# A gate's row sums: from the seam between two stages into the attention heads, in half blocks

## The chip, the cores and the metric

The kernel runs on one core of one Trainium2 chip. The metric is the device time of one execution in microseconds (us). Three runs of the kernel before gave 2838.04, 2838.57 and 2839.91 us; their median, 2838.57 us, is the time that the change is compared with. Everything else comes from one more execution that was profiled: it took 2840.08 us, of which the profile shows a span of 2838.3 us from the first to the last instruction.

The engines are named as in the profile: PE is the matmul engine (PEld its weight loads), DVE the vector engine, ACT the scalar engine, POOL is GpSimd, SP the engine from whose queue most transfers are issued.

## The reference

One input `x` (2048 tokens, 1024 features, float32) goes through two attention blocks of 32 heads, 32 wide, and the results are mixed row by row by a gate:

```python
x = A_x
g = _sigmoid((x * gate_w).sum(-1, keepdims=True))     # one number for each token
a = _A_ref(x, A_wqkv, A_wo)     # linear attention: phi(q) (phi(k)^T v) / (phi(q) . sum phi(k)), then @ wo
b = _B_ref(x, B_wqkv, B_wo)     # softmax attention, then @ wo
return g * a + (1 - g) * b
```

with `phi(t) = where(t > 0, t + 1, exp(t)) + 1e-6`. The gate's sum over 1024 features is a small part of the arithmetic: 2 million products against the matmuls of two attention blocks.

## The kernel before, in words

Every matmul operand of the projections is split into a high and a low part, and three products replace one (`three`, lines 151 to 157: high times high, high times low, low times high). Tokens are cut into 16 blocks of 128 (`NT`), features into pieces of 512 (`C`).

The work has these stages, by the time in the profile:

- **0 to about 400 us, the first stage.** The softmax block's queries, keys and first values are projected, split and stored to DRAM; a split copy of `x` goes to DRAM as `xs`.
- **about 400 to 525 us, the seam.** The remaining value chunk of the softmax block (`kind == "v"` in `linear`) is projected in 16 units of one token block. Each unit needs 1 MB of `xs` from DRAM (`load_half`: half a unit at a time into three halves of `big4` and `xh`), gives one store of values (`v_out`), and the row maxima of the first head start (`maxima`, the matmul of line 1131 and the DVE reduce of line 1136). The first heads' queries and keys are loaded on POOL's queue (`load_first`), their values with `load_v`, a gather of rows of 128 bytes.
- **525 to about 1720 us, the heads along the linear attention's keys and values** (`kind == "kv"`, 64 units), **to about 2120 us along its queries** (`"q"`), and then **along its output** (`"o"`). For each of the 32 heads, scores are computed twice: once with tokens on partitions for the row maxima (line 1131, reduced by DVE on line 1136), once transposed (line 1305) and put through Exp by ACT (line 1308) into a tile of 2048 columns; line 1462 multiplies these with the values. The rows' sums of the probabilities are added up by POOL, in adds of 1536 columns (lines 1393 and 1397), and for the last 512 columns by DVE in a PSUM bank (lines 1411 and 1413).
- **to the end, the output** projection of the softmax block and the mix.

All engine orders are written by a planner in the kernel: `T[...]` holds a planned time for each engine, `use(engine, cost)` advances it, streams (`lin`, `max`, `head`, `out`) are Python generators, and the main loop picks the one that can go on at the planned PE time. Small DVE work is put off with `defer(fn, at, cost, rank)` and fitted by `fill` where the planned DVE has room; the lowest rank goes first. Six to seven PSUM banks go round between the matmuls and their readers (`take`, `give`). SP and each engine execute their own orders strictly in sequence, so an instruction that waits holds up what stands behind it.

The gate, before, is a generator of its own (`gate`, lines 487 to 500), advanced by the seam's units from the third on: it loads the weights (spread over the partitions) into `zrep` on POOL's queue, and then for each of the 16 token blocks a whole block of `x` (128 x 1024, 512 KB), two buffers deep (`big12`), also on POOL's queue. One DVE instruction (line 495) multiplies the block with the weights and puts the row sums into a column of `g_sb`. At the end ACT and DVE make g and 1 - g of it (`omg_sb`). The first reader of `g_sb` is the linear attention's query stage (line 1048), that of `omg_sb` the output (line 1552).

Of the kernel before, what the change touches and what calls it, by code (L numbers as in the profile page):

```python
# [37 lines left out]
SLACK = 0.4  # L38
DMA_ISSUE = 0.45
WARM = 8  # L40
WO_STEP = 4
LATE = 1.0
MANUAL = {ET.PE, ET.DVE, ET.Activation, ET.SP, ET.Pool}
# [4 lines left out]
def kernel(  # L48
# [435 lines left out]
        store(1, 0, U2, H21)  # L484
        next(side, None)

    def gate():
        xn = halves_of(big_tile(12, F32))
        junk = halves_of(big_tile(13, F32))[0]
        nc.gpsimd.dma_start(zrep, bass.AP(tensor=gate_w.tensor, offset=gate_w.offset, ap=[[0, P], [1, D]]))  # L490
        for t in range(NT):
            nc.gpsimd.dma_start(xn[t % 2], x[t * P:(t + 1) * P, :])
            yield
            use("dve", 1.2)
            nc.vector.scalar_tensor_tensor(junk, xn[t % 2], 1.0, zrep, op0=ALU.mult, op1=ALU.mult,
                                           accum_out=g_sb[:, t:t + 1])
        nc.scalar.activation(g_sb, g_sb, AF.Exp, scale=-1.0)
        nc.vector.tensor_scalar_add(g_sb, g_sb, 1.0)
        nc.vector.reciprocal(g_sb, g_sb)
        nc.vector.tensor_scalar(omg_sb, g_sb, -1.0, 1.0, op0=ALU.mult, op1=ALU.add)  # L500

    def halves_of(t):
        return [t[:, i * D:(i + 1) * D] for i in range(2)]
# [429 lines left out]

    def linear():
        extra = iter(())
        gates = gate()
        for n, (i, t) in enumerate(units):
            kind, c = chunks[i]
            follow = chunks[i + 1] if i + 1 < len(chunks) else None
            lag = 2 if kind == "v" else 0  # L940

            def renew(k):

                mark = Later(None, 0.0, 0.0, 0, None)
                w_left[k][:] = [mark]
                next_w.append((follow, k, mark, nc.vector if kind == "v" else nc.gpsimd))
                pump_w(kind == "v")

            yield bank_at
            b = take()  # L950
            ps = bank[b]
            T["pe"] = max(T["pe"], free[b])
            lin_kind[0] = kind
            if (kind, c, t) in (("q", 1, 2), ("q", 1, 8), ("o", 0, 2), ("o", 0, 8)):
                load_mix()
            for k in range(NK):
                yield lambda: ended(w_left[k], w_ready[k], xp_ready.get(2 * n + k // HK, 0.0))
                need(w_left[k])
                if n < TPC:
                    stat = [xpiece(1, xname(0, k % 2), p, k // 2)[:, t * P:(t + 1) * P] for p in range(2)]  # L960
                else:
                    stat = [xstat_lin(n, k, p) for p in range(2)]
                for m, _ in enumerate(three(ps, stat, (wpart(k, 0), wpart(k, 1)), k)):
                    lin_pe(1.0)
                    if m < 2:
                        yield always
                store_mix()
                if kind == "v":
                    if n in (4, 5) and k == 0:
                        load_v(n - 4)  # L970
                    if t > 1 and (k == 3 or k == 7 and t % 2):
                        next(gates, None)
                if n == 1 and k == 0:
                    for m in range(2 * TPC, 2 * TPC + 3):
                        load_half(m)
                if k % HK == HK - 1 and 2 * n + k // HK >= 2 * TPC:
                    load_half(2 * n + k // HK + 3)
                if k == 0 and n + 7 == len(units) and not o_main[0]:
                    load_o(0)
                if k == 1 and n + 1 == len(units):  # L980
                    assert finished[0] >= H - 2
                    need(pr_left[extra_pr[2]])
                    xo_t[0] = big_tile(PR[extra_pr[2]], F32R)
                    split_o(0, slice(0, NK - 1))
                if k == NK // 2 and n + 1 == len(units) and over["head"]:
                    split_o(1, slice(0, NK - 1))
                if k == NK - 1:
                    yield from extra
                if follow and follow[0] == "o":
                    if t == NT - 1:  # L990
                        w_left[k].clear()
                        yield lambda: 0.0 if mixed.count((k // HK, follow[1])) == 8 * HK else None
                        load_wa(follow[1], k)
                    continue
                if follow and t == NT - 2 and k == 0:
                    yield lambda: None if mix_here or stores else 0.0
                if follow and t == NT - 2 and k < min(LEAD_W, NK):
                    coming_w.append(load_w(*follow, k, LEAD_W + 1))
                if follow and t == NT - 1 and k >= lag:
                    renew(k - lag)  # L1000
            extra = iter(())
            e, r = mid[3 + n % 3], mid[6]
            if kind == "v":
                give(b, use("act", 0.5, T["pe"] + LATENCY["pe"]))
                v_out(c, token(i, t), ps, mid[11 - n % 2])
            elif kind == "kv":
                va = mid[7][:, (n % 2) * HC:(n % 2 + 1) * HC]
                yield from keys_alone(n - 2)
                nc.scalar.copy(va, ps[:, HC:])
                use("act", 0.28, T["pe"] + LATENCY["pe"])  # L1010
                end = phi(ps, e, HC)

                def more(end, c=c, t=t, e=e, ps=ps):
                    pk = e[:, :HC]
                    nc.vector.scalar_tensor_tensor(pk, pk, 1.0, ps[:, :HC], op0=ALU.min, op1=ALU.add)
                    z_end[c % 2] = use("pool", 0.69, end)
                    if t == 0:
                        nc.gpsimd.tensor_copy(zsum[c % 2], pk)
                    else:
                        nc.gpsimd.tensor_add(zsum[c % 2], zsum[c % 2], pk)  # L1020

                todo = [defer(more, end, 0.34)]
                give(b, 0.0, todo)
                keys(n, c, t, e, va, todo)
                if t == NT - 1:
                    extra = keysum(c)
            elif kind == "q":
                yield from keys_alone(n - 3)
                yield lambda: None if n - 3 not in turned and chunks[units[n - 3][0]][0] == "q" else 0.0
                end = phi(ps, e, C)  # L1030
                d = dn[n % 2]

                def sums(_, e=e, ps=ps):
                    nc.vector.scalar_tensor_tensor(ps, e, 1.0, ps, op0=ALU.min, op1=ALU.add)

                def scaled(_, c=c, ps=ps, r=r):
                    nc.vector.tensor_mul(r, ps, zrep[:, c * C:(c + 1) * C])

                last = []

                def dens(end, r=r, d=d, last=last):
                    nc.vector.tensor_reduce(d, r.rearrange("p (h d) -> p h d", d=DH), AX.X, ALU.add)
                    nc.scalar.add(d, d, eps)
                    last[0].at = use("act", 0.2, end)

                def divide(_, t=t, e=e, ps=ps, d=d):
                    nc.vector.reciprocal(d, d)
                    nc.vector.scalar_tensor_tensor(
                        e.rearrange("p (h d) -> p h d", d=DH), ps.rearrange("p (h d) -> p h d", d=DH),
                        g_sb[:, t:t + 1], d.unsqueeze(2).to_broadcast([P, C // DH, DH]),  # L1050
                        op0=ALU.mult, op1=ALU.mult)

                todo = chain(((sums, 0.63), (scaled, 0.63), (dens, 0.63), (divide, 0.9)), end)
                last.append(todo[-1])
                give(b, 0.0, todo)
                tasks.append((lambda todo=todo: None if kv_todo else both(ended(todo + o_left), o_free[(len(turned) + 1) % 2], bank_at()),
                              lambda n=n, c=c, t=t, e=e, todo=todo: queries(n, c, t, e, todo)))
            else:
                res = mid[(7, 10)[n % 2]]
                give(b, use("act", 0.5, T["pe"] + LATENCY["pe"]))  # L1060
                nc.scalar.copy(res, ps)
                dma(ra_d[t][:, c * C:(c + 1) * C], res)
            if follow and follow[0] != "o" and t == NT - 1:
                for k in range(NK - lag, NK):
                    renew(k)
# [584 lines left out]
    while streams or tasks:  # L1650
        if not begun[0] and lin_done[0] >= warm and s_done[0] >= NT * NJ + LEAD:
            begun[0] = True
            advance("head")
        pump_w()
        fold_now()
        add_now()
        load_all(False)
# [77 lines left out]
```

## Time and profile before

| | |
|---|---|
| median of three runs | 2838.57 us (2838.04 to 2839.91) |
| the profiled execution | 2840.08 us, span 2838.3 us, mean granted PE clock 0.999 |
| PE busy | 2820.7 us (99%), 15944 matmuls |
| DVE busy | 2231.1 us (79%), 3659 instructions |
| POOL busy | 1936.0 us (68%) |
| ACT busy | 1596.9 us (56%) |
| transfers | 424.36 MB, mean 150 GB/s |

The views used are: the totals by engine; stretches (busy time of each engine between two times, with the granted PE clock, the share of time in which the 16 DMA engines moved packets, and GB/s); groups of instructions by line (busy us, mean ns of one, idle time of the engine just before them and who ended it); waits (who waited for whom, total us, times, longest); the instructions of one tile; and the timeline. Busy time counts an instruction from start to end. Matmuls overlap, so each shows 390 ns although one of 512 columns starts every 0.227 us.

### The profile page before, as it was taken

To read this page: it belongs to the slowest core of one execution; us is meant where nothing else is said; L and a number is where in the kernel's file an instruction comes from. 1 tells how busy PE (TensorE), PEld (TensorE's weight loads), DVE (VectorE), ACT (ScalarE), POOL (GpSimd) and SP (SyncE) were. 2 spreads that over 40 slices of the span, in tenths; PEclk is the share of its full clock that TensorE was granted. 3 is DMA by queue.
4 is the path that set the end of the run, shared out by engine and by line. 5 is a ranking of instruction groups with operands and counts; after the bars stand their busy time and mean duration, and the time that the engine had idled before them with its cause. 6 is when DMAs were issued, how large, how long until landed. Compare 5 with 4: busy or idle time off the path is not lost.

```text
span 2838.3 us, 46552 instructions
## 1 busy us (share of the span) xinstructions
PE 2820.7 (99%) x15944; PEld 2055.4 (72%) x15944; DVE 2231.1 (79%) x3659; ACT 1596.9 (56%) x2994; POOL 1936.0 (68%) x947
## 2 busy tenths in 40 slices
PE   9999999999999999999999999999999999999999
PEld 8888887676677667776777767776766666776787
DVE  7777747788888888888888888778888888887522
ACT  5334320566676667666666666666666656666400
POOL 0000041599999989999999999889889888885000
PEclk9999999999999999999999999999999999999999
DMA  8867768433344334333433344454666455544642
GB/s 274 252 220 231 217 208 283 136 101 103 99 122 109 99 94 127 100 97 105 125 103 102 100 124 142 143 183 161 201 185 174 135 160 142 153 113 129 202 148 78
DMA packets 373928, 424.36 MB, mean 150 GB/s; under 512 B 104750, under 2 KB 210478, under 8 KB 373692
## 3 DMA queue, kind: packets, MB, share of 16 engines
q1 hardware_dynamic: 356396, 396.21, 45.6%
q0 software_dynamic: 17296, 25.17, 4.7%
q8 instruction: 127, 2.08, 0.3%
q14 instruction: 109, 0.89, 0.1%
HBM read 293.86 MB, written 112.98 MB: 143 GB/s over the span
## 4 chain that ended last, share of the span: by engine, by line
PE 97%; DMA 2%; DVE 0%; POOL 0%; ACT 0%; issue 0%; SPq 0%; ACTq 0%; POOLq 0%; DVEq 0%
PE bank L1305 17%; PE bank L1131 16%; PE bank L1462 16%; PE bank L152 15%; PE bank L155 15%; PE bank L157 15%; DMA big<-in_x 1%; PE bank L1196 1%; PE bank L919 1%; PE bank L808 0%; DMA big<-qk 0%; DMA big<-wa 0%; PE bank L1188 0%; DMA extra<-in_a_wqkv 0%; PE bank L879 0%; DMA big<-xs 0%
## 5 line engine op out<-in xcount | busy, mean ns | idle before, releaser
L1397 POOL TENSOR_TENSOR big<-big,big 128x512 f32<-128x512 f32 (+2 forms) x694 | 1644.3, 2373 | 116.5 <-ACT big L1308 74.0
L1136 DVE TENSOR_REDUCE mx<-bank 128x1 f32<-128x512 f32 x2048 | 1304.5, 683 | 254.9 <-PE bank L1131 250.8
L1308 ACT ACTIVATE big<-bank 128x512 f32<-128x512 f32 x2048 | 1179.6, 601 | 431.6 <-PE bank L1305 362.7
L1131 PE MATMUL bank<-big,big 128*128 128x512 f32 x1888 | 740.3, 392 | 2.6 <-ACT big L1308 1.8
L1305 PE MATMUL bank<-big,big 128*128 128x512 f32 x1888 | 742.1, 394 | 0.7 <-ACT mid L355 0.6
L152 PE MATMUL bank<-big,big 128*128 128x512 f32 x1608 | 628.4, 391 | 2.9 <-DMA big<-xs 2.9
L157 PE MATMUL bank<-big,big 128*128 128x512 f32 x1604 | 625.6, 390 | 2.3 <-DMA big<-xs 2.3
L155 PE MATMUL bank<-big,big 128*128 128x512 f32 x1608 | 627.2, 390 | 0.0
L1462 PE MATMUL bank<-big,mid 128*32 128x512 f32 x4096 | 454.1, 593 | 0.0
L1305 PEld LDWEIGHTS bank<-big,big 128*128 128x128 f32 x1888 | 354.0, 188 | 126.5 <-issue 46.9
L1131 PEld LDWEIGHTS bank<-big,big 128*128 128x128 f32 x1888 | 354.7, 188 | 79.0 <-ACT big L1308 5.2
L152 PEld LDWEIGHTS bank<-big,big 128*128 128x128 f32 x1608 | 302.5, 188 | 69.3 <-DMA big<-xs 3.7
L157 PEld LDWEIGHTS bank<-big,big 128*128 128x128 f32 x1604 | 301.3, 188 | 65.6 <-DMA big<-xs 3.2
L155 PEld LDWEIGHTS bank<-big,big 128*128 128x128 f32 x1608 | 302.4, 188 | 63.3 <-DVE big L294 0.2
L1462 PEld LDWEIGHTS bank<-big,mid 128*32 128x32 f32 x4096 | 142.6, 110 | 265.2 <-issue 265.2
L1088 POOL MEMSET big<- 32x512 f32 (+1 forms) x4 | 3.9, 973 | 383.7 <-PE bank L157 383.7
L1413 DVE TENSOR_TENSOR bank<-bank,big 128x512 f32<-128x512 f32 x364 | 251.6, 691 | 5.3 <-ACT big L1308 3.6
L152 PE MATMUL bank<-big,xh 128*128 128x512 f32 x376 | 148.4, 395 | 3.0 <-DMA xh<-xs 2.6
L155 PE MATMUL bank<-big,xh 128*128 128x512 f32 x376 | 147.8, 393 | 0.2 <-DMA big<-wa 0.2
L157 PE MATMUL bank<-big,xh 128*128 128x512 f32 x376 | 147.3, 392 | 0.0
L1393 POOL TENSOR_TENSOR big<-big,big 128x1536 f32<-128x1536 f32 (+1 forms) x31 | 122.8, 3960 | 35.7 <-ACT big L1308 35.7
L1471 ACT COPY mid<-bank 128x512 f32<-128x512 f32 x32 | 18.8, 588 | 207.5 <-PE bank L1462 200.7
(129 smaller groups left out, 2003.4 us busy)
## 6 DMA issues: line engine op xcount, KB each, us to landing
big<-xs SPq DMA_DIRECT2D x288, 256.0 KB
big<-qk SPq DMA_DIRECT2D x690, 64.0 KB
xh<-xs SPq DMA_DIRECT2D x144, 256.0 KB
qk<-mid SPq DMA_DIRECT2D x128, 256.0 KB
big<-oA SPq DMA_DIRECT2D x84, 256.0 KB
xs<-big SPq DMA_DIRECT2D x64, 256.0 KB
oA<-mid SPq DMA_DIRECT2D x64, 256.0 KB
big<-big POOLq DMA_DIRECT2D x50, 256.0 KB, 5.6
```

Source lines behind the costliest of these rows:

```text
L152: yield nc.tensor.matmul(ps, sh, mh_, start=(kt == 0), stop=False)
L155: yield nc.tensor.matmul(ps, sh, ml_, start=False, stop=(late and last))
L157: yield nc.tensor.matmul(ps, sl, mh_, start=False, stop=last)
L919: nc.tensor.transpose(pt[:, i * P:(i + 1) * P], pq[:, i * P:(i + 1) * P], ident)
L1131: nc.tensor.matmul(bank[b], q[:, t % TPC * P:(t % TPC + 1) * P], k[:, j * C:(j + 1) * C], start=True, stop=True)
L1136: nc.vector.tensor_reduce(m[:, t, j:j + 1], bank[b], AX.X, ALU.max)
L1305: nc.tensor.matmul(bank[b], k[:, t * P:(t + 1) * P], q_cols(h, j), start=True, stop=True)
L1308: nc.scalar.activation(pr_t[i][:, j * C:(j + 1) * C], bank[b], AF.Exp, scale=SCALE)
L1393: nc.gpsimd.tensor_add(lacc[:, :qp], pr(0)[:, :qp], pr(1)[:, :qp])
L1397: nc.gpsimd.tensor_add(lacc[:, sl], lacc[:, sl], pr(t)[:, sl])
L1413: nc.vector.tensor_add(lacc[:, qp:] if t == NT - 1 else l_b[:, :n], l_b[:, :n], src)
L1462: nc.tensor.matmul(av_b[j * DH:(j + 1) * DH, :], v[:, t, :], pr(t)[:, j * C:(j + 1) * C], start=(t == 0), stop=(t == NT - 1))
```

## The change: what it does

The generator `gate` and its calls go. A function `gate_step` is called once in each turn of the planner's main loop and acts while the linear stream is in its keys and values. Its first call issues two loads of the weights (128 x 512 each) into `mid8` and `mid9` on SP's queue. Each step then loads one half block of `x` (128 x 512, 256 KB) into `mid10`, also on SP's queue, and defers one DVE instruction to at least 9 us (planned) later, at a planned cost of 0.9 us and with rank 2. It multiplies in place and puts the row sums of the first half into `g_sb`, of the second into `omg_sb`. The next step may come 12 us after that instruction. After 32 steps DVE adds the two halves, and the four instructions that follow are the same as before. `zrep`, `big12` and `big13` are no longer used for the gate.

```diff
+GATE_STEP = 12.0
...
-    def gate():
-        xn = halves_of(big_tile(12, F32))
-        junk = halves_of(big_tile(13, F32))[0]
-        nc.gpsimd.dma_start(zrep, bass.AP(tensor=gate_w.tensor, offset=gate_w.offset, ap=[[0, P], [1, D]]))
-        for t in range(NT):
-            nc.gpsimd.dma_start(xn[t % 2], x[t * P:(t + 1) * P, :])
-            yield
-            use("dve", 1.2)
-            nc.vector.scalar_tensor_tensor(junk, xn[t % 2], 1.0, zrep, op0=ALU.mult, op1=ALU.mult,
-                                           accum_out=g_sb[:, t:t + 1])
-        nc.scalar.activation(g_sb, g_sb, AF.Exp, scale=-1.0)
...
+    gate_w_t = [mid[8], mid[9]]
+    gate_at, gate_n = [0.0], [0]
+
+    def gate_step():
+
+        n = gate_n[0]
+        if lin_kind[0] != "kv" or gate_at[0] is None or gate_at[0] > T["pe"] or n > 2 * NT:
+            return
+        if n == 0:
+            for i, w in enumerate(gate_w_t):
+                dma(w, bass.AP(tensor=gate_w.tensor, offset=gate_w.offset + i * C, ap=[[0, P], [1, C]]))
+        gate_n[0] += 1
+        if n == 2 * NT:
+            nc.vector.tensor_add(g_sb, g_sb, omg_sb)
+            nc.scalar.activation(g_sb, g_sb, AF.Exp, scale=-1.0)
...
+            use("dve", 0.4)
+            return
+        t, i = divmod(n, 2)
+        xn, to = mid[10], (g_sb, omg_sb)[i]
+        dma(xn, x[t * P:(t + 1) * P, i * C:(i + 1) * C])
+        gate_at[0] = None
+
+        def part(end):
+            nc.vector.scalar_tensor_tensor(xn, xn, 1.0, gate_w_t[i], op0=ALU.mult, op1=ALU.mult,
+                                           accum_out=to[:, t:t + 1])
+            gate_at[0] = end + GATE_STEP
+
+        defer(part, T["pe"] + 9.0, 0.9, 2)
...
     def linear():
         extra = iter(())
-        gates = gate()
...
-                    if t > 1 and (k == 3 or k == 7 and t % 2):
-                        next(gates, None)
...
         pump_w()
+        gate_step()
         fold_now()
```

In the built programs the PE has the same instructions before and after. Their order is the same up to the first head's transpose of maxima (profiled at 500 us) and again from the query stage on; between them single instructions change places by a few positions, and in one spot a matmul of a projection by some sixty. DVE has 32 products of 128 x 512 in place of 16 of 128 x 1024, and one add more. POOL's queue loses 17 transfers, SP's gains 34.

More of the change, by code (lines that the diff above doesn't have):

```diff
@@ L485, in quad @@
         next(side, None)
-    def gate():
-        xn = halves_of(big_tile(12, F32))
-        junk = halves_of(big_tile(13, F32))[0]
-        nc.gpsimd.dma_start(zrep, bass.AP(tensor=gate_w.tensor, offset=gate_w.offset, ap=[[0, P], [1, D]]))
-        for t in range(NT):
-            nc.gpsimd.dma_start(xn[t % 2], x[t * P:(t + 1) * P, :])
-            yield
-            use("dve", 1.2)
-            nc.vector.scalar_tensor_tensor(junk, xn[t % 2], 1.0, zrep, op0=ALU.mult, op1=ALU.mult,
-                                           accum_out=g_sb[:, t:t + 1])
-        nc.scalar.activation(g_sb, g_sb, AF.Exp, scale=-1.0)
-        nc.vector.tensor_scalar_add(g_sb, g_sb, 1.0)
-        nc.vector.reciprocal(g_sb, g_sb)
-        nc.vector.tensor_scalar(omg_sb, g_sb, -1.0, 1.0, op0=ALU.mult, op1=ALU.add)
+    gate_w_t = [mid[8], mid[9]]
[11 more added lines that the diff above has]
+            nc.scalar.activation(g_sb, g_sb, AF.Exp, scale=-1.0)
+            nc.vector.tensor_scalar_add(g_sb, g_sb, 1.0)
+            nc.vector.reciprocal(g_sb, g_sb)
+            nc.vector.tensor_scalar(omg_sb, g_sb, -1.0, 1.0, op0=ALU.mult, op1=ALU.add)
+            use("dve", 0.4)
[9 more added lines that the diff above has]
+        defer(part, T["pe"] + 9.0, 0.9, 2)
     def halves_of(t):
@@ L1027, in linear @@
             elif kind == "q":
+                assert gate_n[0] > 2 * NT
                 yield from keys_alone(n - 3)
```

## The prediction

> **What bounds the kernel now.** I read the totals first, then stretches, to find where the PE isn't busy; then its waits there, the transfers behind them, and, for the place that the work moves to, the groups of DVE and POOL.
>
> ```profile
> PE 2820.7 (99%) x15944; PEld 2055.4 (72%) x15944; DVE 2231.1 (79%) x3659; ACT 1596.9 (56%) x2994; POOL 1936.0 (68%) x947
> ...
> core 0: us, PE busy (x) PEld busy (x) DVE busy (x) ACT busy (x) POOL busy (x), PEclk, DMA share, GB/s
> 420.00:450.00 30.00, 23.02 (x84) 17.05 (x83) 10.85 (x18) 2.01 (x4) 4.36 (x9) 0.89 0.92 283
> 450.00:498.00 48.00, 48.00 (x213) 39.74 (x212) 46.35 (x77) 3.53 (x6) 4.23 (x8) 1.00 0.83 275
> 498.00:530.00 32.00, 27.50 (x116) 20.89 (x116) 20.72 (x38) 12.53 (x23) 2.18 (x2) 1.00 0.66 212
> 530.00:1720.00 1190.00, 1189.71 (x7625) 834.89 (x7624) 1035.47 (x1752) 797.05 (x1545) 1116.29 (x555) 1.00 0.39 105
> ```
>
> The PE sets the time: 2820.7 us busy. The change leaves its instructions as they are, so time can come only from gaps. The seam has one from 420 to 450 us, 30 - 23.02 = 6.98 us, with the clock at 0.89 and the transfers at 0.92 of their engines. From 530 us on, along the keys and values, the PE has no gap, DVE is 87% busy (1035.47 of 1190) and POOL 94% (1116.29).
>
> ```profile
> engine line waited for: us in total, times, longest us
> PE bank L152 <- DMA big<-xs: 2.9, 2, 1.6
> PE bank L1131 <- ACT big L1308: 1.8, 1, 1.8
> PE bank L152 <- DMA xh<-xs: 2.6, 1, 2.6
> PE bank L157 <- DMA big<-xs: 2.3, 1, 2.3
> PE bank L1131 <- DVE mx L1136: 0.7, 1, 0.7
> ...
> 420.47 1.06 POOL L492 DMA_DIRECT2D big<-in_x  x2 [0.34 <-issue]
> 428.69 0.53 POOL L492 DMA_DIRECT2D big<-in_x  x1 [7.17 <-DMA big<-in_x]
> ...
> 420.65 1.22 SPq L169 DMA_DIRECT2D mid<-v  x1
> ...
> 429.74 0.57 SPq L169 DMA_DIRECT2D mid<-v  x1
> ...
> L169 SPq DMA_DIRECT2D big<-xs x8: 319/383/7076, 428.3 to 448.5; - x8
> L169 SPq DMA_DIRECT2D xh<-xs x4: 386/410/5622, 422.1 to 438.5; - x4
> ...
> L169 SPq DMA_DIRECT2D big<-xs x167: 319/341/1715, 530.1 to 1685.7; - x167
> L169 SPq DMA_DIRECT2D xh<-xs x84: 319/344/772, 554.3 to 1691.6; - x84
> ```
>
> In the seam the PE waits for `xs`, the operand of its own units. Two of these loads needed 5.6 and 7.1 us only to be issued; in the stage after it, the same loads never need over 1.7. Both stand on SP's queue right behind a gather of values in rows of 128 bytes (`mid<-v`, 420.65 and 429.74 us), while on POOL's queue the gate's blocks of 512 KB run from 420 us on: the transfer engines are shared.
>
> **The seam: what goes.** The gate's 17 transfers leave the seam. The 6.98 us of gap fall away as far as they come from them. To this comes the clock: after the 2.63 us wait the matmuls run at half pace.
>
> ```profile
> 427.35 0.39 PE L157 MATMUL bank<-big,big 128*128 128x512 f32 x1
> 430.38 0.79 PE L152 MATMUL bank<-big,xh 128*128 128x512 f32 x1 [2.63 <-DMA xh<-xs]
> ...
> 433.52 0.54 PE L155 MATMUL bank<-big,xh 128*128 128x512 f32 x1
> 433.90 0.39 PE L157 MATMUL bank<-big,xh 128*128 128x512 f32 x1
> 434.13 0.39 PE L152 MATMUL bank<-big,xh 128*128 128x512 f32 x1
> ```
>
> From 430.38 to 433.90 eight matmuls start, 0.44 us apart; from 433.90 to 434.13 it is 0.23. That costs 8 x 0.21 = 1.7 us for such a gap, and the stretch's 0.89 (11% of 30 us) is 3.3 us for all. At most 6.98 + 3.3 = 10.3 us can be won. DVE's 16 products (1220 ns, below) also go; the 0.7 us wait for `mx` L1136 was theirs. What is late next: the gather and the unit's own loads remain, so some of the gap may. I take 9.5 us; the ends are 5 (half of it, if the gather by itself still holds SP up once) and 10.3. The instruction order of the PE is the same up to 500 us, so nothing new comes in between. The waits from 498 to 530 us (4.5 us) are for `xs` beside the next weights and for ACT, when the gate has ended: they stay, earlier by what was won.
>
> **Along the keys and values: what comes.** First, 34 issues on SP's queue. An issue takes 0.34 us (the median of `xs` loads), 12 us in 1190, and each holds up what stands behind it, loads of `xs`, queries, keys and weights, by that much. The transfer share there is 0.39. The first load of `x` waits for the value store from `mid10`, and behind it on SP's queue stand the third head's queries and half a unit of `xs`:
>
> ```profile
> 521.01 0.32 SPq L169 DMA_DIRECT2D v<-mid  x1
> 524.52 0.80 SPq L169 DMA_DIRECT2D extra<-qk  x2
> ```
>
> Those queries were issued 3.5 us after that store already before, since their tile had to come free, so the wait is covered. Without that cover half a unit of `xs` comes a microsecond later, with two halves in hand. Cost: nothing. By the times of their neighbours in the trace, the DVE products stand 5 to 31 us behind the place of their load in the built order, mostly over 8; the loads of twice the size landed in 6.0 us (median) in the full seam:
>
> ```profile
> big<-in_x POOLq DMA_DIRECT2D x16, 512.0 KB, 6.0
> ```
>
>  So DVE waits for none of them. (If it did, all reduces queue behind it.)
>
> Second, 32 DVE products with a read of the accumulator, and these rows are for them, and for what they meet:
>
> ```profile
> L495 DVE SCALAR_TENSOR_TENSOR big<-big,zrep 128x1024 f32<-128x1024 f32 x16 | 19.5, 1220 | 38.5 <-DMA big<-in_x 38.5
> L739 DVE TENSOR_TENSOR big<-mid,big 128x512 fp32r<-128x512 f32 x6 | 4.2, 693 | 9.6 <-ACT big L737 9.6
> ...
> L495 DVE DVE_READ_ACCUMULATOR big<-big,zrep 128x1 f32 x16 | 1.3, 82 | 0.0
> ...
> L1136 DVE TENSOR_REDUCE mx<-bank 128x1 f32<-128x512 f32 x1197 | 756.6, 682 | 140.2 <-PE bank L1131 138.6
> L1413 DVE TENSOR_TENSOR bank<-bank,big 128x512 f32<-128x512 f32 x263 | 181.7, 691 | 2.3 <-ACT big L1308 1.3
> L1206 DVE RECIPROCAL bank<-bank 128x128 f32<-128x128 f32 x72 | 69.4, 964 | 1.8
> L1015 DVE SCALAR_TENSOR_TENSOR mid<-mid,bank 128x256 f32<-128x256 f32 x64 | 26.5, 414 | 3.8 <-ACT bank L790 3.4
> ...
> L1397 POOL TENSOR_TENSOR big<-big,big 128x1536 f32<-128x1536 f32 x188 | 661.7, 3520 | 38.2 <-ACT big L1308 28.0
> L1397 POOL TENSOR_TENSOR big<-big,big 128x512 f32<-128x512 f32 x216 | 276.5, 1287 | 13.0
> L1393 POOL TENSOR_TENSOR big<-big,big 128x1536 f32<-128x1536 f32 x19 | 74.3, 3913 | 7.0 <-ACT big L1308 7.0
> ```
>
> An instruction of 128 x 512 takes 0.69 us and the read 0.08: 0.77, under the planned 0.9, so 0.13 spare. 32 x 0.77 = 25 us fit into DVE's 155 us of idle time, and the planner has set the PE's order for them. By itself that costs the PE nothing.
>
> But each product reads two tiles of SBUF, its block and the weights, while POOL is adding for 94% of the time. Through this whole stage DVE does nothing of the kind: its large groups each have a `bank`, which is PSUM, among the operands; and line 495 ran in the seam, where POOL adds nothing (4.23 us busy in 48, all transfer issues). So no row shows a price. From below it is nothing: L1413, with one SBUF operand, takes 691 ns here, as L739 does with POOL idle. From above, the two take turns: the product starts only when the running add ends. At a random moment the rest of an add is the sum of n d²/2 over 1190 us: 188 x 3.52²/2 + 216 x 1.287²/2 + 19 x 3.913²/2 = 1489, or 1.25 us; 32 x 1.25 = 40 us of DVE. What of this reaches the PE hangs on the banks. I paired the 1197 reduces of L1136 with the next matmul into their bank, in instruction order: half of the matmuls start at most 0.67 us after the reduce's end. With the spare 0.13, what goes over 0.8 us is paid: 188 x 2.72²/2 + 216 x 0.487²/2 + 19 x 3.113²/2 = 813, or 0.68 us; times 32, 22 us. Where DVE idles anyway (138.6 of 1190 us, 12%) it is covered: 19 us stay. Behind the waiting product stand the reduces; behind them the matmuls of L1131 that need their banks, and all else on the PE.
>
> [...]
>
> Gaps of 2.3 us or more I charge with the half clock, after the 2.63 us row: rests over 3.1 us are (188 x 0.42 + 19 x 0.81)/1190 = 8% of 32, 2.5 gaps, 1.7 us each: 4.3 us. [...] POOL waits too, 32 x 0.69 = 22 us of its 74 idle: covered.
>
> Third, the closing add and the four small operations, on 16 columns, under 0.3 us each, with a wait for ACT among them: 1 us, once.
>
> **The sum**, on the profiled 2840.08 us: - 9.5 + 19 + 4.3 + 1 = + 14.8, 2854.9. The median of the runs was 1.5 us under the profiled execution: 2853.4, said as 2853.
>
> **The rivals.**
>
> *Beside each other.* DVE's second operand costs POOL and itself nothing. For: all present DVE forms run undisturbed beside the adds. Against: none of them reads twice from SBUF. Then the seam's 9.5 us are won and the small stage end is paid: 2838.57 - 9.5 + 1 = 2830, faster. It decides at 9.5/32 = 0.3 us of PE time for each product: under that the change wins.
>
> *Partial turns.* Both slow down a little, or the planner's places happen to fall between adds; 0.3 us a product: 2838.57 - 9.5 + 9.6 + 1 = 2840, no change.
>
> *Long waits.* POOL's adds stand in line, and if the product lost against the next add as well, its wait would be 3.5 us longer for each: 32 x 3.5 = 112 us more, 2965. Against: an add and a product of one add's rest is the simpler order, and ACT gates POOL often (28.0 us of waits).
>
> *The seam's loads stay late.* The gather alone then blocks SP: 5 us won instead of 9.5, which moves every case up by 4.5.
>
> **How the numbers follow.** 0.2% of 2838.57 is 5.7 us, about what a measurement here can tell from nothing. Between its ends of 0 and 1.25 us, a product costs more than (9.5 + 5.7)/32 = 0.48 us in six tenths of the interval and less than 0.12 us in one. The lower end is a way of its own, though, so I move weight to it. Turns 0.55; beside 0.28; partial 0.13; long 0.04. Faster 0.28, same 0.13, slower 0.59. The range: low 2828, the whole 10.3 us won and nothing paid; high 2870, turns with no bank slack (40 x 0.88 + 4.3 + 1 - 9.5 = + 31). Long waits lie outside. Turns alone: 2844 to 2870.
>
> **What would show it.** Right: in the seam the waits for `xs` and the clock's 0.89 gone; along the keys and values the new DVE product's idle time before it ended by POOL, or its duration at 2 us and more, and waits of L1131 for `mx` L1136 adding up to some 20 us. Wrong: a product of 0.7 us with POOL's adds at 3.52 us beside it (the first rival), issues of 5 us still there in the seam (the fourth), or DVE waiting for `in_x` (a cost that I set to nothing).

## The result, and the profile after

The changed kernel took 2845.14 us (median, 2842.17 to 2847.33), the kernel before 2839.87 us beside it (2837.35 to 2841.56): a ratio of 1.002, with a 95% interval from 1.0011 to 1.0029. It is slower, as forecast, but by 5.3 us where the forecast said 14.4. The profiled execution took 2845.76 us, 5.7 more than that of before.

The totals of the changed kernel, then its stretches (the same columns as in the prediction):

```profile
PE 2824.3 (99%) x15944; PEld 2051.5 (72%) x15944; DVE 2267.2 (80%) x3692; ACT 1598.1 (56%) x2994; POOL 1937.3 (68%) x930
```
```profile
core 0: us, PE busy (x) PEld busy (x) DVE busy (x) ACT busy (x) POOL busy (x), PEclk, DMA share, GB/s
420.00:450.00 30.00, 30.00 (x134) 24.71 (x133) 15.50 (x23) 2.35 (x4) 0.00 (x0) 1.00 0.73 208
450.00:498.00 48.00, 48.00 (x214) 39.64 (x213) 37.40 (x57) 5.08 (x10) 0.00 (x0) 1.00 0.57 181
...
530.00:1440.00 910.00, 903.40 (x5782) 626.58 (x5784) 822.87 (x1381) 601.21 (x1163) 849.25 (x422) 1.00 0.42 113
1440.00:1500.00 60.00, 57.76 (x340) 38.89 (x333) 51.93 (x90) 35.70 (x71) 56.23 (x28) 0.97 0.37 97
530.00:1720.00 1190.00, 1181.16 (x7548) 819.07 (x7547) 1066.97 (x1792) 782.96 (x1516) 1107.20 (x549) 1.00 0.41 111
```

The seam's gap is gone (30.00 busy at clock 1.00, before 23.02 at 0.89). Along the keys and values the PE now has 8.8 us without a matmul (1190 - 1181.16, before 0.3). DVE is busy 31.5 us longer there than before.

The groups of DVE and POOL along the keys and values, by form, and all products of the gate taken together (shortest, median and longest in ns, first and last start):

```profile
L1152 DVE TENSOR_REDUCE mx<-bank 128x1 f32<-128x512 f32 x1187 | 746.6, 682 | 105.0 <-PE bank L1147 104.0
L514 DVE SCALAR_TENSOR_TENSOR mid<-mid,mid 128x512 f32<-128x512 f32 x32 | 55.3, 1728 | 0.0
...
L1413 POOL TENSOR_TENSOR big<-big,big 128x1536 f32<-128x1536 f32 x187 | 663.0, 3545 | 42.9 <-ACT big L1324 33.0
L1413 POOL TENSOR_TENSOR big<-big,big 128x512 f32<-128x512 f32 x216 | 278.9, 1298 | 13.2
```
```profile
L514 DVE SCALAR_TENSOR_TENSOR mid<-mid,mid x32: 703/1418/3720, 518.3 to 1464.8; 128x512 f32<-128x512 f32 x32
```

A product takes 1728 ns in the mean, not 0.69 us; POOL's adds keep their length (3545 and 1298 ns, before 3520 and 1287). DVE pays for the meeting.

The PE's waits from 420 to 1720 us, and SP's issues from 420 to 450 us:

```profile
PE bank L1147 <- DVE mx L1152: 5.9, 5, 2.2
PE bank L1321 <- DVE kvb L835: 1.7, 1, 1.7
...
PE bank L153 <- DMA big<-xs: 0.9, 1, 0.9
```
```profile
L170 SPq DMA_DIRECT2D big<-xs x12: 319/362/2977, 424.4 to 448.7; - x12
L170 SPq DMA_DIRECT2D xh<-xs x6: 320/382/1135, 421.7 to 441.3; - x6
```

The waits for `xs` have shrunk to 0.9 us and the issues of 5.6 and 7.1 us are gone; of the waits for DVE, that for `mx` has grown (7.4 us in all, before 0.7) and that for `kvb` is new. DVE waits for `in_x` nowhere.

Named waits don't hold all that the PE loses, since a matmul shows 0.39 us and the next starts 0.227 us after it, so that a start late by less than the difference shows no gap. So I count **lost pitch**: for every matmul of 512 columns on the lines of the projections and scores, the time to the next start less 0.227 us, summed by stretch (us; one profiled execution each; the last four are experiments below; of the stretch from 498 to 530 us a difference of 3 us says little, since the changed kernel and close_act execute the same instructions there and lost 6.3 and 9.2):

| stretch | before | changed | no_gate | one_input | cost2 | close_act |
|---|---|---|---|---|---|---|
| 420 to 450 | 11.5 | 0.0 | 1.1 | 1.5 | 0.2 | 0.8 |
| 498 to 530 | 6.2 | 6.3 | 3.8 | 3.7 | 3.6 | 9.2 |
| 530 to 1440 | 11.2 | 23.3 | 11.4 | 12.7 | 17.3 | 22.2 |
| 1440 to 1500 | 0.9 | 5.3 | 0.9 | 4.8 | 0.9 | 1.1 |
| 1500 to 1725 | 2.7 | 2.8 | 2.5 | 2.8 | 10.6 | 3.0 |

Before to changed: -11.5 in the seam, +12.1 where 30 of the 32 products run, +4.4 at the closing (from 1473 us on): +5.2 with the small rest, against 5.3 in the medians.

### The profile page after: what moved, and what is told of

The parts are those of the page before. It is cut to its first block, busy times and chain, and to the rows that moved or that the text cites. A ratio compares the mean times of both kernels' runs of the same rounds, so it can differ in the third digit from the quotient of the medians.

```text
span 2844.0 us, 46559 instructions
## 1 busy us (share of the span) xinstructions
PE 2824.3 (99%) x15944; PEld 2051.5 (72%) x15944; DVE 2267.2 (80%) x3692; ACT 1598.1 (56%) x2994; POOL 1937.3 (68%) x930
## 4 chain that ended last, share of the span: by engine, by line
PE 95%; DVE 4%; DMA 1%; issue 0%; ACT 0%; SPq 0%; ACTq 0%
PE bank L1321 16%; PE bank L1147 16%; PE bank L153 15%; PE bank L156 15%; PE bank L158 15%; PE bank L1478 15%; DVE mx L1152 2%; DVE mid L514 1%; PE bank L937 1%; PE bank L1212 1%; DMA big<-wa 0%; PE bank L826 0%; DVE bank L1222 0%; DVE bank L1429 0%; PE bank L1204 0%
## 5 line engine op out<-in xcount | busy, mean ns | idle before, releaser
L1413 POOL TENSOR_TENSOR big<-big,big 128x512 f32<-128x512 f32 (+2 forms) x694 | 1651.5, 2384 | 122.7 <-ACT big L1324 80.0
L1478 PE MATMUL bank<-big,mid 128*32 128x512 f32 x4096 | 454.1, 593 | 0.0
L1147 PEld LDWEIGHTS bank<-big,big 128*128 128x128 f32 x1888 | 354.9, 188 | 87.2 <-DVE mx L1152 10.4
L1478 PEld LDWEIGHTS bank<-big,mid 128*32 128x32 f32 x4096 | 142.3, 110 | 265.4 <-issue 265.4
```

The costliest lines, as they stand in the source:

```text
L1147: nc.tensor.matmul(bank[b], q[:, t % TPC * P:(t % TPC + 1) * P], k[:, j * C:(j + 1) * C], start=True, stop=True)
L1413: nc.gpsimd.tensor_add(lacc[:, sl], lacc[:, sl], pr(t)[:, sl])
L1478: nc.tensor.matmul(av_b[j * DH:(j + 1) * DH, :], v[:, t, :], pr(t)[:, j * C:(j + 1) * C], start=(t == 0), stop=(t == NT - 1))
```

## The experiments

The theory is that of the prediction: a seam that gains, products that take turns with POOL's adds, a closing that costs something. Its rival is that the two engines run beside each other and the loss is the order's or the transfers'. Differences below are against the runs of before on the same chip (2838.79, 2838.97 and 2838.46 us in the three groups).

**no_gate: the seam by itself.** The gate is left out: g and 1 - g are two constants of 0.5.

```diff
-        if lin_kind[0] != "kv" or gate_at[0] is None or gate_at[0] > T["pe"] or n > 2 * NT:
-            return
+        if n == 0:
+            gate_n[0] = 2 * NT + 1
+            nc.vector.memset(g_sb, 0.5)
+            nc.vector.memset(omg_sb, 0.5)
+        return
```


> The gate is left out: g and 1 - g are set to 0.5 once, no load of x or of the gate's weights for it and no product anywhere. If the seam's gap came from the gate and everything that the change pays comes from the gate's own instructions, the seam from 420 to 450 us has no gap and the stretch along the keys and values is as in the kernel before: some 11.4 us under the kernel before, 2828 us, 17 us under the changed kernel. If the new order of the PE or other things cost the time along the keys and values, it is less: 2833 us or more.

Measured: 2826.02 us, ratio 0.9952 (0.9939 to 0.9964), 12.8 us under before. The seam is worth that much, and 530 to 1440 us is back at 11.4 us of lost pitch.

**one_input: the same place and loads, one operand.** The product becomes a plain sum over the half block; the weights are left out of it.

```diff
-            nc.vector.scalar_tensor_tensor(xn, xn, 1.0, gate_w_t[i], op0=ALU.mult, op1=ALU.mult,
-                                           accum_out=to[:, t:t + 1])
+            nc.vector.tensor_reduce(to[:, t:t + 1], xn, AX.X, ALU.add)
```


> The changed kernel with the same loads, places and planned costs, but each product is replaced by a DVE reduce of the half block alone, one SBUF operand in place of two (the weights are left out of the sums). Taking turns with POOL: the reduces take 0.68 us each, with no add to wait for, DVE gets back some 33 us, and the PE some 12; what stays is the closing's wait: 2833 us. Rival, that DVE's additional time or the 34 transfers on SP's queue cost it: within 2 us of the changed kernel, 2843 or more.

Measured: 2832.22 us, ratio 0.9977 (0.9966 to 0.9987), 6.6 us under before. The sums of this kernel, all of them:

```profile
L514 DVE TENSOR_REDUCE g_sb<-mid x16: 662/674/678, 520.4 to 1419.4; 128x1 f32<-128x512 f32 x16
L514 DVE TENSOR_REDUCE omg_sb<-mid x16: 664/674/677, 556.6 to 1452.9; 128x1 f32<-128x512 f32 x16
```

None of the 32 exceeds 678 ns. With the same loads, places and planned costs, the other instruction makes the difference of 11.8 us (6.6 + 5.3) to the changed kernel: the turns. The plain sum also writes no half block back to SBUF, so the run by itself doesn't say whether the second read or the write takes turns. A row of the changed kernel does: L1225, which writes 128 x 512 to SBUF but reads only one operand from there.

```profile
L1225 DVE TENSOR_TENSOR mid<-mid,bank x18: 686/686/687, 605.4 to 1705.1; 128x512 f32<-128x512 f32 x18
```

It took 687 ns at most, though 13 of the 18 began while POOL was adding. What these rows leave is the second operand: 1728 ns in the mean with it, at most 678 and 687 without. What still separates one_input from no_gate, 6.2 us, is mostly its closing (4.8 us of lost pitch).

**late_close: does DVE's wait for ACT make the closing dear?** The closing in two steps, what follows Exp one step later.

```diff
             nc.scalar.activation(g_sb, g_sb, AF.Exp, scale=-1.0)
+            gate_at[0] = T["pe"] + GATE_STEP
+            return
+        if n == 2 * NT + 1:
             nc.vector.tensor_scalar_add(g_sb, g_sb, 1.0)
```


> The changed kernel, with the closing in two steps: the add and the Exp first, the three DVE operations that need the Exp one step (12 us planned) later. If DVE's one wait of 6.2 us for ACT cost the PE about 4.5 us at 1480 us, that is gone: 2841 us. If the PE's loss there was covered otherwise, no change: 2845.

Measured: 2845.39 us, ratio 1.0021 (1.0012 to 1.003). A miss: DVE's wait is gone, but in its place the PE waited 2.6 us for the maxima at 1494 us. The timeline there, POOL and DVE:

```profile
1492.46 7.57 POOL L1416 TENSOR_TENSOR big<-big,big 128x1536 f32<-128x1536 f32 x2
...
1492.81 3.71 DVE L508 TENSOR_SCALAR omg_sb<-g_sb 128x16 f32<-128x16 f32 x1
1496.43 1.87 DVE L1155 TENSOR_REDUCE mx<-bank 128x1 f32<-128x512 f32 x3
```

The second `tensor_scalar`, on 16 columns, began beside an add of POOL and lasted until 1496.51 us, when that add had just ended (1496.47); the reduces came behind it. So one wait went and another took its place, and the run doesn't show what the wait for ACT costs.

**cost2: the planner told the truth.** The product planned at 2.0 us instead of 0.9.

```diff
-        defer(part, T["pe"] + 9.0, 0.9, 2)
+        defer(part, T["pe"] + 9.0, 2.0, 2)
```


> The changed kernel with the product planned at 2.0 us in place of 0.9, which is above its measured mean of 1.73: the planner then puts less behind it. If the PE loses time because the wait is not in the plan, the loss of some 13 us falls by half or more: 2838 to 2840 us. If the turns cost the PE whatever the plan says, since DVE is nearly full there: 2845 or more.

Measured: 2840.53 us, ratio 1.0006 (0.9997 to 1.0016), 1.6 us over before. From 530 to 1440 us the lost pitch falls from 23.3 to 17.3: half of the turns' price is that the planner didn't know of them. (The products don't fall better here: the rest of the add that they meet is 1.29 us in the mean, 1.18 in the changed kernel.) But from 1500 to 1725 us, where the closing now falls, it rises to 10.6. The timeline there, POOL first (start, length, engine, line):

```profile
1542.78 6.96 POOL L1413 TENSOR_TENSOR big<-big,big 128x1536 f32<-128x1536 f32 x2
...
1543.02 3.25 DVE L503 TENSOR_SCALAR g_sb<-g_sb 128x16 f32<-128x16 f32 x1 [0.28 <-ACT g_sb L502]
1546.31 0.25 DVE L504 RECIPROCAL g_sb<-g_sb 128x16 f32<-128x16 f32 x1
1546.60 3.17 DVE L505 TENSOR_SCALAR omg_sb<-g_sb 128x16 f32<-128x16 f32 x1
```

POOL does two adds back to back. The first `tensor_scalar` of 16 columns lasts until 1546.28 us, as the first add ends (1546.24); the second until 1549.77, as the second add ends (1549.73). The reciprocal between them takes 0.25 us. So a small operation with one operand takes turns here as well (3253 and 3169 ns, 174 in the seam), and in this run that, not the 0.28 us for ACT, is what the closing pays for.

**close_act: the closing without them.** 1 + e and 1 - g go to ACT, one step apart.

```diff
-            nc.vector.tensor_scalar_add(g_sb, g_sb, 1.0)
-            nc.vector.reciprocal(g_sb, g_sb)
-            nc.vector.tensor_scalar(omg_sb, g_sb, -1.0, 1.0, op0=ALU.mult, op1=ALU.add)
...
+            nc.scalar.activation(g_sb, g_sb, AF.Relu, bias=ones[:, :1])
...
+        if n == 2 * NT + 1:
+            nc.vector.reciprocal(g_sb, g_sb)
...
+        if n == 2 * NT + 2:
+            nc.scalar.activation(omg_sb, g_sb, AF.Relu, scale=-1.0, bias=ones[:, :1])
```


> The changed kernel with its closing taken apart: the add of the two halves stays on DVE, then ACT does Exp and 1 + e (a Relu with a bias of 1), one step later DVE does only the reciprocal, one step later ACT does 1 - g. DVE no longer waits for ACT, and the two tensor_scalars of 128 x 16 are gone from DVE. Theory (the closing costs the PE 4 to 5 us because DVE waits 6.2 us for ACT and the tensor_scalars take turns with POOL's adds): 2840 to 2842, no stall of over 2 us between 1440 and 1500 us, pitch excess there about 1 us. Rival (the closing costs nothing by itself; what was lost there is noise of the order): 2845, like the changed kernel and like late_close.

Measured: 2840.46 us, ratio 1.0008 (0.9999 to 1.0017), 2.0 us over before, 3.3 better than the changed kernel by that count. The two intervals overlap a little, so the stretch decides. Its closing:

```profile
1440.00:1500.00 60.00, 60.00 (x387) 40.73 (x386) 54.67 (x95) 38.50 (x77) 58.37 (x29) 1.00 0.38 104
```

The lost pitch there falls from 5.3 to 1.1, as expected. The kernel removes the wait for ACT and the two `tensor_scalar`s together, so it shows what the closing costs, not the share of each.

**cost2_close: both.** The last two edits together.

> The same closing, and the product planned at 2.0 us instead of 0.9. Theory (both small losses are separate and add up): cost2's 2840.5 less the 5.8 us stall at its closing: 2834 to 2836, still above no_gate's 2826 by what the turns cost the PE. Rival (the stall only moves to another place): 2840.

Measured: 2832.93 us, ratio 0.998 (0.9971 to 0.9989), 5.5 us under before and 1 us below the expected range. Against the changed kernel the single edits win 3.7 and 3.3 us, both together 10.8: more than their sum, because cost2 alone had moved the closing to where it cost more. From 1500 to 1725 us the lost pitch is 2.9 here, 10.6 in cost2. So the stall doesn't move elsewhere, and the gate beside POOL can be made to win, about 7 us short of leaving it out (no_gate).

**split: who goes first when an add ends?** Each product in two of 256 columns; the second halves' sums are left out.

```diff
+            for sl, acc in ((slice(0, HC), to), (slice(HC, C), dn[i])):
+                nc.vector.scalar_tensor_tensor(xn[:, sl], xn[:, sl], 1.0, gate_w_t[i][:, sl], op0=ALU.mult, op1=ALU.mult,
+                                               accum_out=acc[:, t:t + 1])
```


> The changed kernel with each product cut into two of 256 columns, one right behind the other (the second halves' sums go to another tile and are left out of the gate). If a product waits for the add that POOL has running, and POOL's next add comes first again before the second, DVE waits for twice as many adds: the first pieces 1.0 us on average, the second ones a whole add (1.3 or 3.5 us): 60 to 80 us more of DVE, and 15 to 30 of the PE: 2860 to 2875 us. If the second piece gets in ahead of POOL's next add, or if the cost is not turns at all but DVE's work: 0.1 us more for each, 2845 to 2849 us.

Measured: 2904.78 us, ratio 1.0237 (1.0222 to 1.0252), 65.8 us over before, far above what was expected. The 64 pieces:

```profile
L515 DVE SCALAR_TENSOR_TENSOR mid<-mid,mid 128x256 f32<-128x256 f32 x64 | 106.4, 1697 | 0.0
```

Half the work, a mean of 1697 ns (1728 for a whole product), twice as often: the first pieces 1.44 us, the second 1.96. The second piece is issued as the first ends and yet finds POOL's next add in its way: 55 of the 64 end 0.28 us after the end of an add. A whole product waited for one add (32 of 32 ended 0.55 us after it in the changed kernel); here the piece behind the first waited for the next add too. DVE pays no more than expected (the 64 together 53 us over the 32 products), the PE far more. Part of that is the clock: it fell to half ten times, for 41 us in all, which by itself is some 20 us (an estimate: half of 41).

**seam_no_loads: which transfers made the seam's gap?** The kernel before with only the first two blocks of `x` loaded; the other products read what is there.

```diff
-            nc.gpsimd.dma_start(xn[t % 2], x[t * P:(t + 1) * P, :])
+            if t < 2:
+                nc.gpsimd.dma_start(xn[t % 2], x[t * P:(t + 1) * P, :])
```


> The kernel before with all its products in the seam, but only the first two blocks of x are loaded; the other products use these two again. If the transfers made the gap, most of the 11.4 us go, as far as the first two blocks and the weights (1.5 MB at 420 us) do not keep it: 2828 to 2832 us. If DVE's products made it (through the reduces behind them), the gap stays: 2837 to 2840.

Measured: 2834.02 us, ratio 0.9985 (0.9975 to 0.9994), 5.0 us under before, between the two ranges. Half: the first 1.5 MB alone, at 420 us, leave 5.3 of 11.5 us of lost pitch.

**seam_late and seam_sp5: the gate left in the seam, but later.** Both begin with the 7th unit instead of the 3rd; seam_sp5 also issues the loads on SP's queue (second part of the diff, and the same for the weights).

```diff
-                    if t > 1 and (k == 3 or k == 7 and t % 2):
+                    if t > 5 and k in (3, 7):
...
-            nc.gpsimd.dma_start(xn[t % 2], x[t * P:(t + 1) * P, :])
+            dma(xn[t % 2], x[t * P:(t + 1) * P, :])
```


> The kernel before, with its gate in the seam but four units later and two blocks a unit (from the seventh unit on, in place of the third). If the gap came from the gate's blocks meeting the two gathers of values on the transfer engines, it goes although the same bytes stay in the seam: 2829 us, 10 us under the kernel before. If the seam is short of bandwidth as a whole, the gap only moves later: 2836 to 2840.

Measured: 2835.97 us, ratio 0.9987 (0.9978 to 0.9996), 2.8 under before: partly a miss, since only 2.8 of the 10 us came and the gap stayed. Its POOL queue and the PE's first wait:

```profile
420.94 0.57 POOL L490 DMA_DIRECT2D zrep<-in_gate_w  x1
```
```profile
PE bank L152 <- DMA xh<-xs: 3.2, 1, 3.2
```

On POOL's queue the loads stand behind nothing that the units pace: the weights leave at 420.94 us although the gate begins with the 7th unit; before, with the 3rd, they left at 419.56.

> The gate of the kernel before, in the seam from the seventh unit on, two blocks a unit, and its loads on SP's queue, where they stand behind the units' own loads and so cannot start at 420 us, as on POOL's queue. If the seam's gap was the meeting of the gate's first blocks with the gathers, the stretch from 420 to 450 us keeps no wait for xs; DVE's products meet no add of POOL there. 2828 to 2832 us. Rival, the seam is short of transfer time as a whole: 2835 to 2839.

Measured: 2829.16 us, ratio 0.9968 (0.9957 to 0.9979), 9.8 under before. This version beats both kernels. Its seam:

```profile
420.00:450.00 30.00, 30.00 (x132) 24.53 (x132) 15.23 (x25) 2.94 (x5) 1.48 (x3) 1.00 0.91 289
450.00:498.00 48.00, 48.00 (x213) 39.37 (x212) 47.51 (x82) 4.00 (x8) 0.00 (x0) 1.00 0.91 319
```

The transfers run at 289 and 319 GB/s, more than before, and the PE has no gap: the gap did not come from the gate's traffic as such. The first load of the gate leaves at 433.8 us, behind both gathers of values. That this, and not the other queue, is what helps, the next run shows.

**seam_sp4: one unit earlier** (`t > 4`).

> The gate of before in the seam, loads on SP's queue, begun one unit earlier than in seam_sp5 (from the 6th). Theory (what cost before its gap was only the overlap of the gate's first loads with the gathers of values at 420 to 445 us): the 6th unit still lies behind the gathers, so 2829, like seam_sp5, or up to 2 us less where the two products that came late at 511 us are done earlier. Rival (the room from 450 us on is all that matters, and an earlier start meets the gathers again): 2832 to 2836.

Measured: 2831.74 us, ratio 0.9978 (0.9968 to 0.9987). The intervals of the two overlap, so the stretch decides: the clock from 420 to 450 us is 0.94 and 4.3 us of pitch are lost there, on SP's queue too. The rival is nearer in mechanism, though 2831.7 lies just below its bound. SP's queue shows the meeting:

```profile
426.19 0.57 SPq L169 DMA_DIRECT2D mid<-v  x1
426.81 3.70 SPq L169 DMA_DIRECT2D zrep<-in_gate_w  x1
430.55 0.43 SPq L169 DMA_DIRECT2D big<-in_x  x1
431.08 0.85 SPq L169 DMA_DIRECT2D big<-xs  x2
```

The gate's weights now stand right behind the second gather, need 3.70 us to be issued, and hold up the unit's `xs`. So the gap comes from the gate's first loads beside the gathers.

## Why the prediction was right in direction and wrong in size

The forecast of +14.4 us was 9.1 too high: the seam gave 3.3 us more than its term, the turns cost 7 less, the half clock 4.3 less, the closing 3.4 to 5.2 more. The direction is partly luck. The measured 5.3 us lie just under the 5.7 that the prediction named as what a measurement can tell from nothing, though the interval (1.0011 to 1.0029) is clear of it; and they hang on the closing, the term priced at 1 us: without its loss (close_act) the kernel is 2.0 us over before, with an interval that includes a ratio of 1.

**The seam: -9.5, measured -12.8** by no_gate's median (-11.5 by lost pitch), above the upper end of 10.3. Gap and half clock are both in it, as said; idle time and clock counted separately gave a tenth less than the count from start to start. By no_gate's own lost pitch, 10.4 us of the 12.8 lie from 420 to 450 us and 2.4 from 498 to 530, where the prediction had the waits stay; of the second figure one execution each is all there is. The fourth rival, that the gather alone keeps the loads late, falls: without the gate's loads an issue behind it still takes up to 2977 ns, but the PE has no gap there.

**The turns: the mechanism right, the price +19, measured +12.** Each of the 32 products ends 0.55 us (0.54 to 0.56) after the end of the add that ran when it began; the mean rest of these adds is 1.18 us, where I had 1.25. That the products take turns was an assumption of the prediction, since no row of the kernel before has such a product beside an add; the trace of the changed kernel shows it in 32 of 32, and one_input's sums, with one operand from SBUF, took 674 ns. The first rival, beside each other, falls. The step that failed is the next one, "32 x 0.68": it charged every product with what goes over 0.8 us. On the real rests that charge gives 17 us, or 15 with the 12% taken off; the PE lost 10.8 us (late starts of over 0.15 us, from a product's start to 5 us after its end). The difference is where they fell. One of the long ones, POOL, DVE and PE:

```profile
982.55 10.92 POOL L1413 TENSOR_TENSOR big<-big,big 128x1536 f32<-128x1536 f32 x3
...
986.83 3.31 DVE L514 SCALAR_TENSOR_TENSOR mid<-mid,mid 128x512 f32<-128x512 f32 x1
990.07 0.08 DVE L514 DVE_READ_ACCUMULATOR mid<-mid,mid 128x1 f32 x1
...
987.46 5.76 PE L1478 MATMUL bank<-big,mid 128*32 128x512 f32 x52
```

The product is held up 2.76 us, but the PE is in a run of 52 matmuls of L1478, probabilities times values, which need no bank from DVE's reduces. The eight products with the longest rests split cleanly. With 40 and more such matmuls beside them: rests 2.62, 2.76, 2.26 and 1.99, losses 0.26, 0.75, 0 and 0 us. With none: rests 3.17, 2.25, 2.33 and 2.78, losses 2.37, 1.27, 1.42 and 1.56. The allowance of 0.8 us was about right where the PE waits for banks; that for stretches it doesn't was missing. I had taken 12% off for DVE's idle time, when it was the PE's other work that covers. That is a pairing in the trace, not an experiment, and a late start of 0.35 us follows the third of the covered ones just behind the 5 us.

**The half clock: +4.3 for 2.5 gaps, measured none for the products.** From 530 to 1440 us the granted clock is 1.00 and no matmul runs at half pace. It did come once, at the closing: the PE's timeline there.

```profile
1482.14 0.50 PE L1321 MATMUL bank<-big,big 128*128 128x512 f32 x1 [1.72 <-DVE kvb L835]
...
1484.07 0.80 PE L1147 MATMUL bank<-big,big 128*128 128x512 f32 x1 [0.52 <-DVE mx L1152]
1484.66 0.63 PE L1321 MATMUL bank<-big,big 128*128 128x512 f32 x1
...
1487.22 0.47 PE L1147 MATMUL bank<-big,big 128*128 128x512 f32 x1
1487.53 0.40 PE L1321 MATMUL bank<-big,big 128*128 128x512 f32 x1
```

After 1.72 and 0.52 us of idle time, eight matmuls need 3.46 us (1484.07 to 1487.53) instead of 1.82. The term fell because its gaps never came: the rests did not reach the PE whole. The nearest, 2.21 us at 523 us behind the first product, brought no half clock either; what decides it besides the length of the gap was not shown.

**The closing: +1, measured 4.4.** 1.72 + 0.52 us of idle time and 1.6 us of half pace are 3.9 of it. DVE there:

```profile
1473.27 0.57 DVE L501 TENSOR_TENSOR g_sb<-g_sb,omg_sb 128x16 f32<-128x16 f32 x1
1480.06 0.42 DVE L503 TENSOR_SCALAR g_sb<-g_sb 128x16 f32<-128x16 f32 x1 [6.23 <-ACT g_sb L502]
1480.52 0.25 DVE L504 RECIPROCAL g_sb<-g_sb 128x16 f32<-128x16 f32 x1
1480.80 0.90 DVE L505 TENSOR_SCALAR omg_sb<-g_sb 128x16 f32<-128x16 f32 x1
```

Two steps failed. The larger in this kernel is the wait for ACT, which the prediction put inside its 1 us: DVE stood idle for 6.23 us, and `kvb` and the reduces came late behind it. The other is "under 0.3 us each": the 174 ns of a `tensor_scalar` come from the seam, where POOL adds nothing. I had looked for operations with two SBUF operands alone; cost2 shows 3.25 us for one with a single operand, late_close 3.71, each until an add ends. So the 691 ns of L1413, with one operand from SBUF beside the adds, did not carry over to these.

**The rest held.** SP's 34 issues, the loads of `x` and POOL's own time cost nothing that shows. What was measured, -12.8 (no_gate) + 6.2 (closing and rest) + 11.8 (turns) = 5.2, is the result by construction, as each term is the difference between two kernels in the row; the lost pitch by stretch is the count that does not come from the medians. The price of a product is 12/32 = 0.38 us of PE time, just above the 0.3 us from which the prediction let the change lose; the second rival's 0.3 us, "partial turns", would have been nearer the number, by a mechanism that isn't there.

## What to carry to other kernels

Before DVE work is moved beside a busy POOL, look at each instruction's operands, the tiny ones too: those that took turns with POOL here (the products with two SBUF operands, and the `tensor_scalar`s) paid the rest of a running add, in the mean 1728 ns for products of 512 columns and 1697 for pieces of 256, up to 3707 for 16 columns. So one big instruction was better than two small ones (5.3 us over before against 65.8 in split), and the planner must be told that cost. What reached the PE was that wait less the slack of its banks (1.27 to 2.37 us of rests of 2.25 to 3.17), and little or nothing where the PE had work that needs none of them (0 to 0.75 us of rests of 1.99 to 2.76): read that from what the PE executes there, not from an average. And before work is moved out of a crowded stage, try moving it by a few units within it, on a queue that is paced by the work around it.

## What the runs showed of the hardware

- In split, 55 of the 64 pieces of a product end 0.28 us after the end of an add of POOL; the first pieces take 1.44 us in the mean, the second, right behind them, 1.96.
- A `tensor_scalar` of 128 x 16 took 3253 and 3169 ns beside POOL's adds, 160 and 3707 ns in late_close, 418 and 900 ns in the changed kernel, 174 ns in the seam.
- The half clock doesn't follow from the length of a gap alone. It came after 2.63 us in the kernel before, after 1.72 and 0.52 us in the changed kernel and after 2.16 us in close_act (at 525 us), and did not come after 3.40 us in split (at 1488 us), 2.67 us in close_act (at 509 us) or 2.21 us in the changed kernel (at 523 us). What decides it was not shown: no run was made to test it.
- From 20 to 2836 us, the granted clock was 0.50 from 430.41 to 433.82 and from 444.06 to 447.48 us in the kernel before, and from 1483.96 to 1487.37 us in the changed kernel: 3.41 us each time.
